# q of two batches loaded in runs of four tokens, with the scores and exponentials that undo the order

## The chip, the cores and the metric

The kernel runs on one core of one Trainium2 chip. The metric is the device time of one execution in microseconds, as the median over several runs. The engines are TensorE (matmuls, PE in the profile; its weight loads are PEld), VectorE (DVE), ScalarE (ACT), GpSimd (POOL) and SyncE (SP, which here only issues DMAs).

## The reference

Sliding-window attention with a linear distance bias, then a two-layer network with a hard swish. Batch 8, 8 heads, 576 tokens, head size 64; the network goes 512 to 2048 to 512 over 4608 tokens.

```python
def _attn_ref(q, k, v):
    B, H, S, D = q.shape                       # 8, 8, 576, 64
    scores = 1.0 / np.sqrt(D) * np.matmul(q, k.transpose(0, 1, 3, 2))
    rel = np.arange(S)[:, None] - np.arange(S)[None, :]
    slopes = 2.0 ** (-8.0 * (np.arange(H) + 1) / H)
    bias = slopes[:, None, None] * (-np.abs(rel))[None]
    mask = (rel >= 0) & (rel < 128)
    scores = np.where(mask, scores + bias[None], -1e9)
    attn = np.exp(scores - scores.max(-1, keepdims=True))
    return np.matmul(attn / attn.sum(-1, keepdims=True), v)

def _moe_ref(x, w_in, w_out):                  # x: (4608, 512), heads side by side
    h = x @ w_in
    return (h * np.clip(h + 3.0, 0.0, 6.0) / 6.0) @ w_out
```

q, k, v and the weights come as float32, the result is float32.

## The kernel before

**Work.** Attention runs in 32 groups: group g is batch g // 4 and one pair of heads, g % 4. The network runs in 9 blocks of 512 tokens; of each, 16 up steps (four matmuls into `hps`, L562, or eight half as wide, then a Relu on ScalarE, L581, and a product on VectorE, L582, into `gbuf`) and 16 down steps (four matmuls into `ops`, L619; after four steps a copy, L628, and a store). The up steps of a block wait for the attention of its tokens. `hps` has two PSUM banks, `ops` one, the attention values `av` one, and the scores `sce` the two tiles of two banks that are left.

**Order.** Every engine runs its instructions in the order in which they are written. Until group 13 a script names each step (`SCRIPT`: `ldq:3:1` loads block 1 of q of batch 3, `ct:3:q` casts it, `xb:3:q` transposes it, `S:12` is the scores of group 12, `ed` and `eo` the exponentials, `v` the values, `F` one step of the network). After that a loop over `slot(g)` writes the scores of group g, then two exponentials of the diagonal, the values of group g - 1, the exponentials beside the diagonal, with network steps between them.

**How q gets to the scores.** From batch 3 on, q (and from batch 4 on, k) is loaded as tokens by SP (`load_tokens`, L140): block j of 128 tokens goes to `ldbuf`, one token to a partition, in eight runs of 256 B, one for each head. The fifth block has the last 64 tokens. GpSimd casts each block to bf16 into `tbuf` (`cast_tokens`, L222), two heads to a pair. SP then transposes all of it by one DMA (`xbar`, L227) into `qTb`: on the partitions the 64 values of two heads, in the columns the 576 tokens of a pair of heads.

**Scores and probabilities.** The scores of a group are taken transposed, keys on the partitions. For each block j of 128 keys, tile `sce[e]` (one for each head of the pair) holds 256 columns: the 128 queries of the same block ("s = 0", the diagonal) and the 128 of the next one ("s = 1"). So that nothing outside the window is computed, each block of keys is cut in four strips of 32, and each strip has a matmul with the 160 queries that can see it (L393; fewer at the end of the sequence), in a tile of 64 x 32 of the array, of which eight run side by side. The last 64 keys have two strips (L400). ScalarE takes the exponentials: of the diagonal into `pd` (L417), of the next block into `po` (L441) and of the last 64 queries' diagonal into `p4buf` (L446); its bias carries the distance term of the key. GpSimd clears what lies outside the window with `affine_select` (L434, L443, L449), which counts columns as tokens. The matmuls of `values` (L462, L470) take `pd`, `po` and `p4buf` as weights, column by column a token. Batches 0 and 1 go other ways, and group 8 has wider score matmuls (L365, L370).

Of the kernel before, what the change touches and what calls it, by code (L numbers as in the profile page):

```python
# [14 lines left out]
ACT = mybir.ActivationFunctionType  # L15
# [3 lines left out]
def kernel(  # L19
# [9 lines left out]
    nc = tc.nc  # L29
    B, H, S, D = q.shape  # L30
# [4 lines left out]
    scale = 1.0 / (D ** 0.5)  # L35
    NP = H // 2
    NQ = 5
    LAST = S - 4 * 128
# [23 lines left out]
    bias_d = perm.tile([128, H], FP32)  # L62
# [23 lines left out]
    src_of = {"q": q, "k": k, "v": v}  # L86
# [43 lines left out]
    def tokens(b, nm):  # L130
        if (b, nm) not in ld:
            i = 2 + b % 2 if b < 3 else (3, 1, 0, 2)[(3 * (b - 3) + "qkv".index(nm)) % 4]
            ld[b, nm] = ldbuf[i][:, 0:NQ * H * D].rearrange("p (j h d) -> p j h d", j=NQ, h=H)
        return ld[b, nm]

    def load_tokens(b, nm, blocks=range(NQ), eng=nc.sync):
        t = tokens(b, nm)
        for j in blocks:
            n = min(128, S - j * 128)
            eng.dma_start(out=t[:n, j, :, :],  # L140
                              in_=src_of[nm][b, :, ds(j * 128, n), :].rearrange("h p d -> p h d"))

# [65 lines left out]
    def staged(b, nm):  # L208
        return tbuf[int(b > 3 and nm == "k")]

    def cast_tokens(b, nm):
        s = ld[b, nm]
        if nm == "v":
            for lo in (0, 2):
                nc.gpsimd.tensor_copy(  # L215
                    out=vbuf[b % 2][:, lo:lo + 2, :, 0:D].rearrange("p j h d -> p (j h) d"),
                    in_=s[:, lo:lo + 2, :, :].rearrange("p j h d -> p (j h) d"))
            nc.gpsimd.tensor_copy(out=vbuf[b % 2][:LAST, 4, :, 0:D], in_=s[:LAST, 4, :, :])
            return
        for j in range(NQ):  # L220
            m = min(128, S - j * 128)
            nc.gpsimd.tensor_copy(out=staged(b, nm)[:m, :, j, :],  # L222
                                  in_=s[:m, j, :, :].rearrange("p (i e) d -> p i (e d)", e=2))

# [5 lines left out]
    st = {}  # L230
# [59 lines left out]
    def full(g):  # L290
        return g < NB_FULL * NP

    def diag_tabled(g):
        return g < NP
# [9 lines left out]
    def rooms(g):  # L304
        b, hp = divmod(g, NP)
        if full(g):
            room = w_out_sb if b == 0 else gbuf[1]
            for i, nm in enumerate(("pd", "po")):
                st[g, nm] = room[:, ds(4 * hp + 2 * i, 2), :].rearrange(
                    "p e (j c) -> p e j c", j=4)  # L310
        else:
            st[g, "pd"] = ppool.tile([128, 2, 4, 128], BF16, tag="pd", name="pd")
            st[g, "po"] = ppool.tile([128, 2, 4, 128], BF16, tag="po", name="po")

    def scores_diag(g):
        rooms(g)
        b, hp = divmod(g, NP)
        qT, kT = qTb[b % 2][:, hp, :, :], kTb[b % 2][:, hp, :, :]
        first = not diag_tabled(g)
        if (g, "scd") not in st:  # L320
            tables_diag(g)
        scd = st[g, "scd"]
        for j in range(4):
            for e in range(2):
                r = slice(e * D, (e + 1) * D)
                nc.tensor.matmul(scd[:, e, ts(j, 128)], lhsT=kT[r, j, :],  # L326
                                 rhs=qT[r, j, :], start=first, stop=first or j == 3)
# [15 lines left out]
    def scores_off(g):  # L343
        b, hp = divmod(g, NP)
        qT, kT = qTb[b % 2][:, hp, :, :], kTb[b % 2][:, hp, :, :]
        foff = not full(g)
        if (g, "sco") not in st:
            tables_off(g)
        sco = st[g, "sco"]
        for e in range(2):  # L350
            r = slice(e * D, (e + 1) * D)
            nc.tensor.matmul(sco[:, e, 64:128], lhsT=kT[r, 4, :],
                             rhs=qT[r, 4, 0:LAST], start=foff, stop=foff)
        for j in range(4):
            n = 128 if j < 3 else LAST
            for e in range(2):
                r = slice(e * D, (e + 1) * D)
                nc.tensor.matmul(sco[:, e, ds((j + 1) % 4 * 128, n)], lhsT=kT[r, j, :],
                                 rhs=qT[r, j + 1, 0:n], start=foff, stop=foff or j == 3)
    def scores_whole(kT, qT, sce):  # L360
        for j in range(4):
            for e in range(2):
                r = slice(e * D, (e + 1) * D)
                n = min(256, S - 128 * j)
                nc.tensor.matmul(  # L365
                    sce[e][:, j, :, :].rearrange("p s c -> p (s c)")[:, 0:n],
                    lhsT=kT[r, j, :], rhs=qT[r, ds(128 * j, n)], start=True, stop=True)
        for e in range(2):
            r = slice(e * D, (e + 1) * D)
            nc.tensor.matmul(sce[e][:, 3, 1, 64:128], lhsT=kT[r, 4, :], rhs=qT[r, 512:S],  # L370
                             start=True, stop=True)

    def scores(g):
        if full(g):
            scores_diag(g)
            scores_off(g)
            return
        rooms(g)
        b, hp = divmod(g, NP)
        qT = qTb[b % 2][:, hp, :, :].rearrange("p j c -> p (j c)")  # L380
        kT = kTb[b % 2][:, hp, :, :]
        if g == 2 * NP:
            st["sce"] = [ps_sc.tile([128, 4, 2, 128], FP32, tag="sc", name="sce")
                         for _ in range(2)]
            scores_whole(kT, qT, st["sce"])
            return
        sce = st["sce"]
        for j in range(4):
            for lo in range(0, 128, 32):
                n = min(160, S - 128 * j - lo)  # L390
                for e in range(2):
                    r = slice(e * D, (e + 1) * D)
                    nc.tensor.matmul(  # L393
                        sce[e][lo:lo + 32, j, :, :].rearrange("p s c -> p (s c)")[:, ds(lo, n)],
                        lhsT=kT[r, j, lo:lo + 32], rhs=qT[r, ds(128 * j + lo, n)],
                        start=True, stop=True)
        for lo in range(0, LAST, 32):
            for e in range(2):
                r = slice(e * D, (e + 1) * D)
                nc.tensor.matmul(sce[e][lo:lo + 32, 3, 1, 64 + lo:128],  # L400
                                 lhsT=kT[r, 4, lo:lo + 32], rhs=qT[r, 512 + lo:S],
                                 start=True, stop=True)
# [10 lines left out]
    def exp_diag(g, e):  # L413
        h = 2 * (g % NP) + e
        pd = st[g, "pd"]
        if not full(g):
            nc.scalar.activation(out=pd[:, e, :, :], in_=st["sce"][e][:, :, 0, :],  # L417
                                 func=ACT.Exp, bias=bias_d[:, h:h + 1], scale=scale)
            mask_diag(g, e)
            return  # L420
        sc = st[g, "scd"]
        if diag_tabled(g):
            if e == 0:
                nc.scalar.activation(out=pd.rearrange("p e j c -> p e (j c)"), in_=sc,
                                     func=ACT.Exp, scale=scale)
            return
        nc.scalar.activation(out=pd[:, e, :, :].rearrange("p j c -> p (j c)"),
                             in_=sc[:, e, :], func=ACT.Exp,
                             bias=bias_d[:, h:h + 1], scale=scale)
        mask_diag(g, e)  # L430
# [7 lines left out]
    def exp_off(g, e):  # L438
        h = 2 * (g % NP) + e
        po, sc, p4 = st[g, "po"], st["sce"][e], p4buf[g % 2]  # L440
        nc.scalar.activation(out=po[:, e, :, :], in_=sc[:, :, 1, :], func=ACT.Exp,  # L441
                             bias=bias_o[:, h:h + 1], scale=scale)
        nc.gpsimd.affine_select(out=po[:, e, :, :], in_=po[:, e, :, :],  # L443
                                pattern=[[0, 4], [-1, 128]], channel_multiplier=1, base=-1,
                                compare_op=ALU.is_ge, fill=0.0)
        nc.scalar.activation(out=p4[:, e, 0:64], in_=sc[:, 3, 1, 64:128], func=ACT.Exp,  # L446
                             bias=bias_d[:, h:h + 1], scale=scale)
        if e == 1:
            nc.gpsimd.affine_select(out=p4[:, :, 0:64], in_=p4[:, :, 0:64],  # L449
                                    pattern=[[0, 2], [1, 64]], channel_multiplier=-1, base=0,  # L450
                                    compare_op=ALU.is_ge, fill=0.0)
# [190 lines left out]
    at = [0]  # L642
# [236 lines left out]
```

## Time and profile before

| | |
|---|---|
| median of 3 runs | 319.1 us (318.49 to 319.7) |
| the profiled execution's own time | 318.45 us |
| its span, first to last instruction | 316.7 us |
| granted TensorE clock | 1.0 throughout |
| busy share of the span | PE 97%, PEld 52%, DVE 56%, ACT 61%, POOL 44% |
| read from and written to memory | 36.70 MB, 9.44 MB |

The profile is of one execution. Busy times count overlapping instructions of an engine once; a matmul's own duration is longer than the step to the next one, as matmuls are pipelined. A row of instructions reads: line, engine, operation, output<-inputs, shape, xcount | busy us, mean ns of one | idle us before them and what ended it. A row of the timeline starts with the start and the duration in us, and merges neighbours of one kind; a bracket at its end would be idle time before it and what ended that. A row of waits has the total, the number and the longest. A row of the chain in order of time has start and duration. In the slices each digit is the busy tenth of 1/40 of the span. A row of DMA issues ends with the KB of one and the median us from issue to landing (a transpose's row shows only the latter).

### The profile page before, as it was taken

The numbers are of one execution on the slowest core, as the hardware profiler recorded it, in microseconds if no ns is written. First come the engines' busy times: TensorE is split into PE (matmuls) and PEld (weight loads), VectorE is DVE, ScalarE is ACT, GpSimd is POOL, SyncE is SP. The second block draws the span as 40 slices with busy tenths as digits, with TensorE's granted clock in tenths as the row PEclk, the third lists the DMA queues.
The fourth block names the chain that finished last, engine by engine and source line by source line (L and its number), as shares of the span: only waits on it lengthen the run. The fifth ranks groups of instructions, "written<-read, shape, count | busy, mean of one in ns | idle before, by whom it ended". The sixth has DMA issues, their size and how long they took to land.

```text
span 316.7 us, 7831 instructions
## 1 busy us (share of the span) xinstructions
PE 308.1 (97%) x3143; PEld 165.7 (52%) x3143; DVE 177.2 (56%) x345; ACT 193.9 (61%) x331; POOL 139.3 (44%) x246
## 2 busy tenths in 40 slices
PE   7879999999999999999999999999999999999996
PEld 6565465555555455544677644455444444444443
DVE  6667585666645655565565556555656455455510
ACT  3758968866857766776677666766774244244401
POOL 8455493456777377636763676363230000000000
PEclk9999999999999999999999999999999999999999
DMA  7999999999999999999999999932212100000112
GB/s 279 198 331 221 265 256 198 232 249 195 184 176 212 213 222 245 227 231 224 207 207 216 205 206 204 218 94 56 57 41 70 54 34 35 33 33 35 66 59 73
DMA packets 131428, 51.95 MB, mean 164 GB/s; under 512 B 118976, under 2 KB 123328, under 8 KB 131392
## 3 DMA queue, kind: packets, MB, share of 16 engines
q1 hardware_dynamic: 126160, 45.36, 69.2%
q0 software_dynamic: 4224, 4.19, 8.3%
q10 hardware_dynamic: 1008, 1.90, 1.7%
q8 instruction: 24, 0.39, 0.5%
q14 instruction: 12, 0.10, 0.1%
HBM read 36.70 MB, written 9.44 MB: 146 GB/s over the span
## 4 chain that ended last, share of the span: by engine, by line
PE 90%; DMA 3%; DVE 2%; POOL 2%; ACT 1%; SPq 1%; issue 0%; POOLq 0%
PE hps L562 39%; PE ops L619 39%; PE sce L393 3%; DMA ldbuf<-in_q_dram 3%; PE av L470 2%; PE av L462 2%; PE tp L261 1%; PE ops L593 1%; DVE avs L493 1%; DVE gbuf L582 1%; PE sco L337 1%; PE scd L326 1%; SPq L126 1%; PE tp L246 0%; ACT w_out_sb L405 0%
## 5 line engine op out<-in xcount | busy, mean ns | idle before, releaser
L581 ACT ACTIVATE r<-hps,bias 128x512 f32<-128x512 f32 x144 | 99.0, 689 | 88.7 <-PE hps L562 88.5
L582 DVE SCALAR_TENSOR_TENSOR gbuf<-r,hps 128x512 bf16<-128x512 f32 x144 | 98.7, 687 | 94.6 <-ACT r L581 93.2
L562 PE MATMUL hps<-xT,w_in_sb 128*128 128x512 bf16 (+1 forms) x640 | 144.4, 358 | 0.3 <-ACT xT L549 0.3
L619 PE MATMUL ops<-w_out_sb,gbuf 128*128 128x512 bf16 x560 | 138.3, 379 | 0.0
L562 PEld LDWEIGHTS <-w_in_sb 128*128 128x128 bf16 x640 | 59.4, 98 | 55.1 <-DMA w_in_sb<-in_moe_w_in_dram 0.4
L619 PEld LDWEIGHTS <-gbuf 128*128 128x128 bf16 x560 | 51.7, 98 | 55.3
L443 POOL TENSOR_SCALAR_AFFINE_SELECT po<-po 128x512 bf16<-128x512 bf16 x48 | 30.5, 637 | 44.4 <-ACT po L441 44.4
L434 POOL TENSOR_SCALAR_AFFINE_SELECT pd<-pd 128x512 bf16<-128x512 bf16 x48 | 29.9, 635 | 31.9 <-ACT pd L417 31.8
L417 ACT ACTIVATE pd<-sce,bias_d 128x512 bf16<-128x512 f32 x48 | 31.8, 685 | 5.6 <-POOL tbuf L222 3.9
L628 DVE COPY osb<-ops 128x512 f32<-128x512 f32 x33 | 22.7, 687 | 22.3 <-PE ops L619 22.2
L441 ACT ACTIVATE po<-sce,bias_o 128x512 bf16<-128x512 f32 x48 | 32.9, 686 | 0.1
L222 POOL CAST tbuf<-ldbuf 128x512 bf16<-128x512 f32 (+1 forms) x45 | 25.6, 615 | 0.1
L481 DVE TENSOR_TENSOR avs<-av,rc 128x384 bf16<-128x384 f32 (+1 forms) x48 | 23.5, 490 | 1.6
L470 PEld LDWEIGHTS <-pd 128*128 128x128 bf16 x192 | 14.3, 97 | 7.4 <-POOL pd L434 0.2
L462 PE MATMUL av<-vbuf,po 128*128 128x65 bf16 x192 | 18.0, 193 | 0.0
L470 PE MATMUL av<-vbuf,pd 128*128 128x65 bf16 x192 | 17.3, 194 | 0.0
L462 PEld LDWEIGHTS <-po 128*128 128x128 bf16 x192 | 14.4, 98 | 2.4
L446 ACT ACTIVATE p4buf<-sce,bias_d 128x64 bf16<-128x64 f32 x48 | 15.4, 321 | 0.0
L253 POOL CAST pr<-ldbuf 128x576 bf16<-128x576 f32 x16 | 10.5, 672 | 7.2 <-DMA ldbuf<-in_k_dram 5.3
L215 POOL CAST vbuf<-ldbuf 128x1024 bf16<-128x1024 f32 x12 | 12.2, 1044 | 2.3 <-DMA ldbuf<-in_v_dram 2.3
L393 PEld LDWEIGHTS <-kTb 64*32 64x32 bf16 x736 | 6.2, 91 | 8.3 <-issue 8.1
L393 PE MATMUL sce<-qTb,kTb 64*32 64x160 bf16 (+1 forms) x736 | 10.5, 229 | 0.0
(104 smaller groups left out, 215.1 us busy)
## 6 DMA issues: line engine op xcount, KB each, us to landing
out_dram<-osb SPq DMA_DIRECT2D x33, 256.0 KB, 2.9
ldbuf<-in_v_dram SPq DMA_DIRECT2D x32, 256.0 KB, 4.9
ldbuf<-in_q_dram SPq DMA_DIRECT2D x20, 256.0 KB, 5.0
ldbuf<-in_k_dram SPq DMA_DIRECT2D x16, 256.0 KB, 4.5
ldbuf<-in_q_dram SPq DMA_DIRECT2D x12, 288.0 KB, 6.8
ldbuf<-in_k_dram SPq DMA_DIRECT2D x12, 288.0 KB, 6.2
w_in_sb<-in_moe_w_in_dram POOLq DMA_DIRECT2D x4, 512.0 KB, 9.4
w_out_sb<-in_moe_w_out_dram POOLq DMA_DIRECT2D x4, 512.0 KB, 10.5
```

The source lines that it names most:

```text
L222: nc.gpsimd.tensor_copy(out=staged(b, nm)[:m, :, j, :], in_=s[:m, j, :, :].rearrange("p (i e) d -> p i (e d)", e=2))
L393: nc.tensor.matmul(sce[e][lo:lo + 32, j, :, :].rearrange("p s c -> p (s c)")[:, ds(lo, n)], lhsT=kT[r, j, lo:lo + 32], rhs=qT[r, ds(128 * ...
L417: nc.scalar.activation(out=pd[:, e, :, :], in_=st["sce"][e][:, :, 0, :], func=ACT.Exp, bias=bias_d[:, h:h + 1], scale=scale)
L434: nc.gpsimd.affine_select(out=pd[:, e, :, :], in_=pd[:, e, :, :], pattern=[[0, 4], [1, 128]], channel_multiplier=-1, base=0, compare_op=AL ...
L441: nc.scalar.activation(out=po[:, e, :, :], in_=sc[:, :, 1, :], func=ACT.Exp, bias=bias_o[:, h:h + 1], scale=scale)
L443: nc.gpsimd.affine_select(out=po[:, e, :, :], in_=po[:, e, :, :], pattern=[[0, 4], [-1, 128]], channel_multiplier=1, base=-1, compare_op=A ...
L462: nc.tensor.matmul(out_av, lhsT=po[:, e, qt % 4 if full(g) else qt - 1, :], rhs=vb[:, qt - 1, h, :], start=True, stop=False)
L470: nc.tensor.matmul(out_av, lhsT=d, rhs=vb[:, qt, h, :], start=(qt == 0), stop=True)
L562: nc.tensor.matmul(hps[:, lo:hi], lhsT=w_in_sb[:, ks, ts(ms, 128)], rhs=xT[:, ks, ds(src, hi - lo)], start=(ks == 0), stop=(ks == n_ks - 1))
L581: nc.scalar.activation(out=r6, in_=hps, func=ACT.Relu, bias=bias3[:, 0:1], scale=1.0 / 6.0)
L582: nc.vector.scalar_tensor_tensor(out=gts[nt][:, ms, :], in0=r6, scalar=1.0, in1=hps, op0=ALU.min, op1=ALU.mult)
L619: nc.tensor.matmul(ops[nt, sub], lhsT=gts[nt][:, ms, ts(sub, 128)], rhs=w_out_sb[:, ms, :], start=(ms == 0), stop=(ms == n_ms - 1))
```

## The change

For batches 3 and 4, blocks 0 to 3 of q are loaded differently. DMA j now brings heads 2j and 2j + 1, and partition a gets tokens 4a to 4a + 3 of each, which lie together in memory: two runs of 1 KB for a partition. The cast takes block j to head pair j, ordered by token within the four, then head. After the transpose, the first 512 columns of `qTb` are ordered t, a for token 4a + t. The fifth block (64 tokens) is loaded, cast and transposed as before.

The scores read q^T by fours: a strip's queries are four runs of up to 40 columns, and go to four runs of the 256 columns of its block in `sce`, where a column now stands at t x 64 + a. Queries from 512 on, which lie in token order, are read every fourth column to the same layout, in matmuls of their own: 44 matmuls to a group, where there were 36. The exponentials read `sce` as a, t, neighbours 64 float32 apart, and write `pd`, `po` and `p4buf` in token order, so that masks and values stay as they are. The script and the order of the steps are unchanged.

```diff
+    FOURS = (3, 4)
+
+    def by_fours(b, nm):
+        return b in FOURS and nm == "q"
+
     def load_tokens(b, nm, blocks=range(NQ), eng=nc.sync):
         t = tokens(b, nm)
         for j in blocks:
             n = min(128, S - j * 128)
+            if by_fours(b, nm) and j < 4:
+                eng.dma_start(out=t[:, j, :, :].rearrange("p (e t) d -> p e (t d)", e=2),
+                              in_=src_of[nm][b, 2 * j:2 * j + 2, 0:512, :].rearrange(
+                                  "e (a t) d -> a e (t d)", t=4))
+                continue
             eng.dma_start(out=t[:n, j, :, :],
                               in_=src_of[nm][b, :, ds(j * 128, n), :].rearrange("h p d -> p h d"))
 ...
+            if by_fours(b, nm) and j < 4:
+                nc.gpsimd.tensor_copy(
+                    out=staged(b, nm)[:, j, 0:4, :].rearrange("p t (e d) -> p t e d", e=2),
+                    in_=s[:, j, :, :].rearrange("p (e t) d -> p t e d", e=2))
+                continue
 ...
+    def fours(ap):
+        return ap.rearrange("p (a t) -> p t a", t=4)
+
+    def scores_fours(kT, qT, sce):
+        q4 = qT[:, 0:512].rearrange("p (t a) -> p t a", t=4)
+
+        def block(e, j, lo, at, src):
+            r = slice(e * D, (e + 1) * D)
+            to = sce[e][lo:lo + 32, min(j, 3), :, :].rearrange(
+                "p s c -> p (s c)").rearrange("p (t a) -> p t a", t=4)
+            nc.tensor.matmul(to[:, :, ds(at, src.shape[-1])], lhsT=kT[r, j, lo:lo + 32],
+                             rhs=src[r], start=True, stop=True)
+
+        for j in range(4):
+            for lo in range(0, 128, 32):
+                n = min(160, 512 - 128 * j - lo)
+                for e in range(2):
+                    block(e, j, lo, lo // 4, q4[:, :, ds((128 * j + lo) // 4, n // 4)])
+        for lo in range(0, 128, 32):
+            for e in range(2):
+                block(e, 3, lo, 32, fours(qT[:, ds(512, min(32 + lo, LAST))]))
+        for lo in range(0, LAST, 32):
+            for e in range(2):
+                block(e, 4, lo, 48 + lo // 4, fours(qT[:, 512 + lo:S]))
+
+    def part(sc, g, s):
+        if g // NP not in FOURS:
+            return sc[:, :, s, :]
+        return sc.rearrange("p j s c -> p j (s c)").rearrange(
+            "p j (t a) -> p j a t", t=4)[:, :, ds(32 * s, 32), :]
+
+    def whole(out, g):
+        return out if g // NP not in FOURS else out.rearrange("p j (a t) -> p j a t", t=4)
 ...
-            nc.scalar.activation(out=pd[:, e, :, :], in_=st["sce"][e][:, :, 0, :],
+            nc.scalar.activation(out=whole(pd[:, e, :, :], g), in_=part(st["sce"][e], g, 0),
                                  func=ACT.Exp, bias=bias_d[:, h:h + 1], scale=scale)
 ...
-        nc.scalar.activation(out=po[:, e, :, :], in_=sc[:, :, 1, :], func=ACT.Exp,
+        nc.scalar.activation(out=whole(po[:, e, :, :], g), in_=part(sc, g, 1), func=ACT.Exp,
                              bias=bias_o[:, h:h + 1], scale=scale)
 ...
-        nc.scalar.activation(out=p4[:, e, 0:64], in_=sc[:, 3, 1, 64:128], func=ACT.Exp,
-                             bias=bias_d[:, h:h + 1], scale=scale)
+        nc.scalar.activation(out=whole(p4[:, e:e + 1, 0:64], g),
+                             in_=part(sc[:, 3:4, :, :], g, 1)[:, :, 16:32, :] if g // NP in FOURS
+                             else sc[:, 3:4, 1, 64:128], func=ACT.Exp, bias=bias_d[:, h:h + 1], scale=scale)
```

More of the change, by code (lines that the diff above doesn't have):

```diff
@@ L387, in scores @@
         sce = st["sce"]
+        if b in FOURS:
+            scores_fours(kT, qT, sce)
+            return
         for j in range(4):
```

## The prediction

> **What bounds the kernel now.** I read the slices of the page and its chain first, then what TensorE waited for in the part of the run that the change touches.
>
> ```profile
> PE   7879999999999999999999999999999999999996
> ACT  3758968866857766776677666766774244244401
> DMA  7999999999999999999999999932212100000112
> PE 90%; DMA 3%; DVE 2%; POOL 2%; ACT 1%; SPq 1%; issue 0%; POOLq 0%
> ```
>
> TensorE and the DMA engines are both full from slice 2 to slice 26, so both are candidates. The chain says which: 90% of it is TensorE and 3% is DMA. I place that 3% next. Asked for the waits of TensorE's matmuls from 50 us to the end, the view names none; for its weight loads it names three:
>
> ```profile
> PEld L393 <- issue: 8.1, 20, 0.4
> PEld L562 <- issue: 0.2, 1, 0.2
> PEld L470 <- POOL pd L434: 0.2, 1, 0.2
> ```
>
> No DMA and no q among them. "Issue" is no wait on another engine (the weight loads of the scores get ahead and sit there), so 0.2 us, behind a mask, is all the waiting for somebody else. The DMA share is one early stretch, long before:
>
> ```profile
> 14.75 8.04 DMA ldbuf<-in_q_dram
> ```
>
> When do the changed parts run? The timeline gives the first and last of the eight score groups of batches 3 and 4, the q cast of batch 3, and its transpose:
>
> ```profile
> 72.57 2.84 POOL L222 CAST tbuf<-ldbuf 128x512 bf16<-128x512 f32 x5
> 75.44 3.42 SPq L227 DMA_TRANSPOSE qTb<-tbuf  x1
> 83.17 0.46 PE L393 MATMUL sce<-qTb,kTb 64*32 64x160 bf16 x32
> 134.99 0.46 PE L393 MATMUL sce<-qTb,kTb 64*32 64x160 bf16 x32
> sum 64.00, PE 64.00 PEld 32.39 DVE 35.68 ACT 44.86 POOL 42.03; mean PE 8.00 PEld 4.05 DVE 4.46 ACT 5.61 POOL 5.25
> ```
>
> The last row sums eight stretches of 8 us from 83 to 147 us: TensorE busy 64.00 of 64.00, ScalarE 5.61 of each 8. So in this stage the matmul stream itself sets the end. What the change takes off the DMA queues buys nothing; what it adds to TensorE is paid in full; what it adds to ScalarE is paid only where a matmul comes to wait for it.
>
> **The loads.** The eight changed q loads (four blocks of two batches, 128 x 8 runs of 256 B each) have 8,192 packets; as 1 KB runs they have 2,048.
>
> ```profile
> DMA packets 131428, 51.95 MB, mean 164 GB/s; under 512 B 118976, under 2 KB 123328, under 8 KB 131392
> q1 hardware_dynamic: 126160, 45.36, 69.2%
> q0 software_dynamic: 4224, 4.19, 8.3%
> ```
>
> A packet of q1, nearly all of 256 B, takes 0.692 x 16 x 316.7 us / 126,160 = 27.8 ns. One of q0, about 1 KB, takes 0.083 x 16 x 316.7 / 4,224 = 99.6 ns. Between a 1 KB packet at 99.6 and at 27.8 ns the change frees (8,192 x 27.8 - 2,048 x 99.6)/16 = 1.5 us to 6,144 x 27.8/16 = 10.7 us on each DMA engine. Worth in time: nothing, as no matmul here waits for a transfer. The loads keep their places in SP's queue; what stands behind them there (other loads, transposes, stores) can only issue earlier if the loads are quicker. Were one slower, the cover is this: the five casts at 72.57 ran without waiting for a DMA.
>
> **The cast and the transpose.** The cast keeps five instructions of 128x512. Its input goes from flat to runs of 64, its output from four runs to one. Rows for both kinds, and the transposes' landing:
>
> ```profile
> L222 POOL CAST tbuf<-ldbuf 128x512 bf16<-128x512 f32 x36 | 20.6, 616 | 0.0
> L218 POOL CAST vbuf<-ldbuf 64x512 bf16<-64x512 f32 x6 | 3.7, 613 | 2.4 <-DMA ldbuf<-in_v_dram 2.4
> qTb<-tbuf SPq DMA_TRANSPOSE x5, 6.9
> ```
>
> L218 writes runs of 64 (65 apart) and takes 613 ns against 616, so I take no change. The transpose of batch 3, issued at 75.44, should land near 82.3, 0.8 us ahead of the first score group at 83.17; the cast may grow by 0.8 us (a quarter) before that group waits. Groups follow each other every (134.99 - 83.17)/7 = 7.4 us, so batch 4's first scores come 30 us later, and its q is loaded right behind this transpose: there the room is wider.
>
> **The scores.** One old group among the dense matmuls:
>
> ```profile
> 126.06 1.03 PE L562 MATMUL hps<-xT,w_in_sb 128*128 128x512 bf16 x4
> 127.02 0.46 PE L393 MATMUL sce<-qTb,kTb 64*32 64x160 bf16 x32
> 127.31 0.19 PE L400 MATMUL sce<-qTb,kTb 64*32 64x64 bf16 x4
> 127.43 1.04 PE L619 MATMUL ops<-w_out_sb,gbuf 128*128 128x512 bf16 x4
> ```
>
> A group has 36 matmuls; the new one has 44, because block 3's queries split into those of the fours and the last 64. The columns are the same: per head 3 x 4 x 160 + (160 + 160 + 128 + 96) + 96 = 2,560 before, 1,920 + (128 + 96 + 64 + 32) + (32 + 64 + 64 + 64) + 96 = 2,560 after. The 32 take 127.31 - 127.02 = 0.29 us, 9 ns each, so eight more cost between nothing (columns decide) and 0.072 us (count decides): over eight groups 0 to 0.6 us. A gain is excluded, as nothing is removed. I take the middle, 0.3 us, since block 3's short pieces leave parts of the array unequally loaded. That the outputs now go to four runs of 40 columns, and some inputs are read every fourth element, no row shows; the trace has no matmul with a broken output. From below it costs 0, from above I take a doubling (rival two).
>
> **The exponentials.** They read PSUM in runs of four, neighbours 256 B apart, to write token order. There is a near row: ScalarE's copies of transposes read PSUM just so (neighbours 128 bf16, 256 B, apart), in runs of 9, 5 or 4.
>
> ```profile
> L441 ACT ACTIVATE po<-sce,bias_o 128x512 bf16<-128x512 f32 x48 | 32.9, 686 | 0.1
> L549 ACT COPY xT<-tb 128x576 bf16<-128x576 bf16 x6 | 3.9, 647 | 4.0 <-PE tb L544 4.0
> L405 ACT ACTIVATE gbuf<-sco 128x1024 bf16<-128x1024 f32 x4 | 4.1, 1026 | 0.1
> L286 ACT COPY qTb<-tp 128x1152 bf16<-128x1152 bf16 x1 | 1.1, 1119 | 0.0
> L274 ACT COPY kTb<-tp 128x640 bf16<-128x640 bf16 x4 | 3.0, 753 | 1.7 <-PE tp L261 1.7
> L274 ACT COPY kTb<-tp 128x512 bf16<-128x512 bf16 x2 | 1.4, 720 | 0.0
> L446 ACT ACTIVATE p4buf<-sce,bias_d 128x64 bf16<-128x64 f32 x48 | 15.4, 321 | 0.0
> ```
>
> The flat reads L549 and L405 give (1026 - 647)/448 = 0.846 ns per element, so flat would be 1134 at 1152, 701 at 640, 593 at 512. Runs of 9 (L286) took 1119: the stride alone costs nothing. Runs of 5 took 753, +52; runs of 4 took 720, +127. The new exponentials have 128 runs of 4, as the last row has, so +0.13 us each (686 to 815 ns), with 0 as the lower end (the excess could come from L274's broken output; the new output is flat). p4's 16 runs add 16 ns to 321. Per group 4 x 0.13 + 2 x 0.016 = 0.55 us, 4.4 us over eight groups; ScalarE goes from 5.61 to 6.2 of each 8 us. The Trainium skill speaks against this edit: "Advanced Engine Details and Errata", section PSUM Cachelines, says every two consecutive elements should be contiguous for best throughput, and these never are. The L286 row disagrees, as it ran at the flat rate with neighbours 256 B apart.
>
> Does a matmul come to wait? The tightest places, in order of time:
>
> ```profile
> 96.17 0.32 ACT L446 ACTIVATE p4buf<-sce,bias_d 128x64 bf16<-128x64 f32 x1
> 96.88 0.46 PE L393 MATMUL sce<-qTb,kTb 64*32 64x160 bf16 x32
> 129.96 0.68 ACT L417 ACTIVATE pd<-sce,bias_d 128x512 bf16<-128x512 f32 x1
> 130.53 0.69 ACT L441 ACTIVATE po<-sce,bias_o 128x512 bf16<-128x512 f32 x1
> 131.40 0.69 ACT L581 ACTIVATE r<-hps,bias 128x512 f32<-128x512 f32 x1
> 132.12 0.69 DVE L582 SCALAR_TENSOR_TENSOR gbuf<-r,hps 128x512 bf16<-128x512 f32 x1
> 133.17 1.03 PE L562 MATMUL hps<-xT,w_in_sb 128*128 128x512 bf16 x4
> ```
>
> The next scores overwrite the PSUM tiles that the last exponential read: 96.49 to 96.88 leaves 0.39 us. And an up-projection reuses the bank that VectorE left at 132.81: 0.36 us ahead of 133.17. At that second place two exponentials and one p4 run back to back ahead of the Relu, together 0.28 us late: about 0.1 us is left, near what a semaphore takes. So at 0.13 us I get no stall. I carried longer ones through the rows of the eight groups (each instruction starts at its old time, or when what precedes it on its engine or what it waits for is done): the stalls add up to 0.5 us at 0.20 per exponential, 1.3 at 0.25, 2.1 at 0.30 and 4.6 at 0.43. The edge is near 0.13.
>
> **The sum.** Loads 0, casts 0, scores +0.3, exponentials 0 on the path. The profiled execution took 318.45 us (1.75 outside its span of 316.7), so 318.75; the median of the runs, 319.1, is 0.65 above that execution, so the median after is 319.4.
>
> **The rivals.** One, slower by ScalarE: reading fp32 in runs of four costs more than the bf16 copies show. It decides from about 0.27 us per exponential; at 0.30 the sum is +2.4 us, 321.5; at half rate (+0.43, 512 more element times at 0.846) +4.9, 324.0. For: fp32 is no row there. Against: L286's full rate. Chance 0.16.
>
> Two, slower by TensorE: broken outputs double the score rounds, 8 x 0.29 = 2.3 us more, 321.7. Nothing in the trace excludes it. The Trainium skill, "PSUM — Partial Sum Buffer", Specifications, says that any non-contiguous pattern slows matmuls significantly; no run here shows it, and runs of 160 bytes break it only at their ends. Chance 0.08.
>
> Three, faster: the freed DMA time counts after all, by easing the traffic beside TensorE's reads. By the chain:
>
> ```profile
> 145.57 1.73 PE ops L619 x8
> 299.79 10.36 PE ops L619 x48
> ```
>
> Eight in 1.73 us amid full DMA and 48 in 10.36 us with hardly any are both 216 ns each. There is nothing to ease. If all of the least saving, 1.5 us, came off, 317.6. Chance 0.03.
>
> Four: the run stays split in 256 B packets; then the loads change nothing and the time is the forecast's. Chance 0.02. The forecast itself has 0.71.
>
> **How the numbers follow.** About 0.5% (1.6 us) is what a measurement can tell from no change. Same: forecast and rival four, and 0.02 of rival one below its point, 0.75 in all, of which I give 0.03 to sums just over the bound: 0.72. Faster 0.03, slower 0.25. The range starts 0.9 below the old median (the runs spread 1.2 us) and goes up to 322.2, which holds rivals one at 0.30 and two, and leaves out only the half rate.
>
> **What would show it.** Right: total packets down by 6,144, those under 512 B by 8,192; 64 more score matmuls; the 32 exponentials near 815 ns; still no wait of a matmul past 50 us. Wrong: score groups spanning 0.6 us or more, exponentials above 0.9 us with matmuls of the scores (on L446) or of the up-projection (on L582) waiting between 83 and 147 us, or a cast over 0.75 us.

## The result and the profile after

The changed kernel takes 320.95 us (median; 319.95 to 321.96) against 318.84 us of the kernel before: ratio 1.0065, interval 1.0047 to 1.0083. It lies inside the stated range, but on its slower side, past the bound of 0.5% (which the interval still reaches); the forecast itself was 319.4. The profiled execution took 320.95 us, its span is 319.2, 2.5 us more than before.

The page after: packets, fetches of instructions, and the chain.

```profile
DMA packets 125285, 51.97 MB, mean 163 GB/s; under 512 B 110784, under 2 KB 117184, under 8 KB 125248
q8 instruction: 25, 0.41, 0.6%
PE 84%; DMA 6%; DVE 3%; POOL 2%; issue 2%; ACT 1%; POOLq 0%
```

The loads do what they say: 8,192 fewer small packets, 6,143 fewer in all (6,144 and one more fetch of instructions). The chain has lost TensorE's share, and part of it went to DMA. The waits of TensorE's matmuls from 50 us on, none before, are now:

```profile
PE ops L672 <- issue: 1.8, 11, 0.2
PE hps L615 <- DMA xT<-avs: 1.4, 2, 0.7
PE hps L615 <- issue: 0.2, 1, 0.2
```

"Issue" is gaps in the records: 42 of 3,207 matmuls are missing in this profile, none in that of before. The second row is real: twice an up step waits for a transpose into xT, the attention output that the network reads. The timeline has the two places, the first and last score group of batches 3 and 4, and one of them among its neighbours:

```profile
83.40 0.56 PE L398 MATMUL sce<-qTb,kTb 64*32 64x160 bf16 x44
127.72 0.56 PE L398 MATMUL sce<-qTb,kTb 64*32 64x160 bf16 x44
135.77 0.56 PE L398 MATMUL sce<-qTb,kTb 64*32 64x160 bf16 x44
155.91 1.14 PE L615 MATMUL hps<-xT,w_in_sb 128*128 128x256 bf16 x9 [0.74 <-DMA xT<-avs]
188.61 1.24 PE L615 MATMUL hps<-xT,w_in_sb 128*128 128x512 bf16 x5 [0.62 <-DMA xT<-avs]
```

From the first to the last score group it is 52.37 us, against 51.82 before: 0.55 over seven groups, 0.079 us each, so 0.6 us for eight. The two waits have 1.4 us. The first score group starts 0.23 us later than before, a difference that is there at 30 us already, while the first changed load is issued at 61 us, so that no edit reaches it. 0.6 + 1.4 + 0.2 = 2.2 of the 2.5 us. The other 0.3 comes at the two waits, which cost more than the idle time that the rows show: from the score group before each to the one behind it, the stream falls back by 0.90 and 0.78 us against before.

ScalarE and GpSimd, grouped by shape, between 83 and 147 us (the last row over the whole run):

```profile
L469 ACT ACTIVATE pd<-sce,bias_d 128x512 bf16<-128x512 f32 x18 | 12.0, 684 | 1.8 <-PE sce L398 1.8
L493 ACT ACTIVATE po<-sce,bias_o 128x512 bf16<-128x512 f32 x16 | 11.0, 685 | 0.0
L498 ACT ACTIVATE p4buf<-sce,bias_d 128x64 bf16<-128x64 f32 x17 | 5.5, 321 | 0.0
L233 POOL CAST tbuf<-ldbuf 128x512 bf16<-128x512 f32 x8 | 4.6, 612 | 0.0
```

The exponentials that pick single elements 256 B apart out of PSUM take 684 to 685 ns, what the flat ones took; the casts take 612.

### The profile page after: what moved, and what is told of

Its sections match the earlier page's. It is cut to its first block, busy times and chain, and to the rows that moved or that the text cites. A ratio compares the mean times of both kernels' runs of the same rounds, so it can differ in the third digit from the quotient of the medians.

```text
span 319.2 us, 7917 instructions
## 1 busy us (share of the span) xinstructions
PE 304.6 (95%) x3165; PEld 165.5 (52%) x3207; DVE 177.6 (56%) x345; ACT 194.1 (61%) x331; POOL 139.1 (44%) x246
## 4 chain that ended last, share of the span: by engine, by line
PE 84%; DMA 6%; DVE 3%; POOL 2%; issue 2%; ACT 1%; POOLq 0%
PE hps L615 37%; PE ops L672 36%; DMA w_in_sb<-in_moe_w_in_dram 3%; DMA xT<-avs 3%; PE av L523 2%; PE av L515 2%; PE sce L445 2%; PE sce L398 1%; PE ops L646 1%; DVE avs L546 1%; PE tp L276 1%; PE scd L341 1%; PE sco L352 1%; DVE gbuf L635 1%; DVE kTb L262 1%
## 5 line engine op out<-in xcount | busy, mean ns | idle before, releaser
L672 PE MATMUL ops<-w_out_sb,gbuf 128*128 128x512 bf16 x533 | 134.0, 379 | 2.5 <-issue 1.8
L237 POOL CAST tbuf<-ldbuf 128x512 bf16<-128x512 f32 (+1 forms) x37 | 21.1, 615 | 0.0
L533 DVE RECIPROCAL rc<-av 128x6 f32<-128x6 f32 (+1 forms) x48 | 8.7, 182 | 1.7 <-PE av L523 1.7
L276 PE MATMUL tp<-ident,pr 128*128 128x128 bf16 x90 | 7.4, 219 | 0.2
```

Of the source, the lines that this page charges most:

```text
L672: nc.tensor.matmul(ops[nt, sub], lhsT=gts[nt][:, ms, ts(sub, 128)], rhs=w_out_sb[:, ms, :], start=(ms == 0), stop=(ms == n_ms - 1))
```

## The experiments

A first guess is that the loads, having become other traffic, hold up the transposes (theory A of the first four runs); the rival is that the wait comes with what is added to the scores. The first four kernels part the change.

**Loads alone.**

```diff
         sce = st["sce"]
-        if b in FOURS:
-            scores_fours(kT, qT, sce)
-            return
...
-            nc.scalar.activation(out=whole(pd[:, e, :, :], g), in_=part(st["sce"][e], g, 0),
+            nc.scalar.activation(out=pd[:, e, :, :], in_=st["sce"][e][:, :, 0, :],
```

> Only the loads and the casts of q of batches 3 and 4 go by fours; scores and exponentials are those of before, so the order is not put back and the output of these two batches is of mixed tokens. Theory A (the loads move the DMA traffic so that the transposes into xT land later and the up-projection waits for them): no step in the score groups, but stalls before the up steps that need batches 4 and 5, about 1.5 us in all, ratio 1.004 to 1.005, and a spread of the runs as wide as that of after (2 us). Theory B (the loads are hidden and the stalls come with TensorE's added time): ratio 1.000, no wait of a matmul for xT.

Measured: 319.0 us, ratio 0.9969 (0.9952 to 0.9986). One wait for xT of 0.68 us at 155 us, none near 188. Theory A falls: the loads by themselves cost nothing, and perhaps bring 0.3%, beyond what theory B expected (which had no wait for xT either). Its profile does not show from where; the kernel of before ran at 0.9989 on the same chip (below), so a part of it may be the chip's scatter.

**Scores and exponentials alone.**

```diff
     def by_fours(b, nm):
-        return b in FOURS and nm == "q"
+        return False
```

> Only the scores and exponentials go by fours; q is loaded and cast as before, so the scores read wrong queries and the output of batches 3 and 4 is not the reference's. Both theories: eight steps of 0.08 us in the PE stream, one at each group, 0.62 us. Theory A: nothing more, ratio 1.002. Theory B: the stalls for xT as well, ratio 1.006.

Measured: 322.51 us, ratio 1.0083 (1.0053 to 1.0113). Waits for xT of 0.93 us at 158.7 and 0.65 us at 191.4. So the second wait and at least a part of the loss come with this half. Not all of it: the profiled execution (323.8 us) is 2.8 us behind that of before at 30 us already, where no edit is, and the runs spread from 320.53 to 325.29.

**Before and after once more,** unchanged.

> The kernel of before, unchanged. If the stalls for xT are chance of an execution and not of the change, this profile can show one too and its runs spread by 1.5 us or more; if they belong to the change, ratio 1.000 and no matmul waits for xT.

Measured: 319.58 us, ratio 0.9989 (0.9968 to 1.001). One wait for xT, at 155.3 us, 0.94 us; none near 188. The place at 155 us is therefore on the edge in the kernel of before as well: the first profile of it had no wait there, this one has.

> The changed kernel again. Ratio 1.0065 and again 0.62 us in eight steps; if the stalls for xT are a matter of single executions, they stand at other places or have another size in this profile than the 0.74 and 0.62 us of the first one, with the same 0.62 us of steps.

Measured: 321.87 us, ratio 1.0063 (1.0039 to 1.0088). Waits of 1.75 us at 157.1 and 0.61 us at 189.8. The second wait is the same as in the first profile to 0.01 us: it is no chance. What makes it? The transpose itself is longer. The DMA view of the stretch in which the last transpose of batch 5 is in flight, before (182 to 185.1 us) and after (184 to 188.6 us); the last number of the xT row is the time from issue to landing:

```profile
q1 hardware_dynamic: 1118, 0.50, 68.2%
q14 instruction: 1, 0.01, 0.6%
xT<-avs SPq DMA_TRANSPOSE x1, 2.8
```

```profile
q1 hardware_dynamic: 2661, 0.78, 73.6%
q8 instruction: 1, 0.02, 1.4%
xT<-avs SPq DMA_TRANSPOSE x1, 4.6
```

In after, a packet of queue q8 lies inside. q8 fetches instructions, 16 KB at a time: 24 fetches before, 25 after, one about every 256 instructions of TensorE (6,286 matmuls and weight loads before, 6,414 after: the 64 matmuls added and their 64 weight loads). q14 fetches instructions too, 8 KB at a time and in about 0.3 us; one of its packets lies in four of the six short flights of the table below, so such a packet does not by itself lengthen a flight so far. So a new theory A: the count of instructions shifts the points of the fetches, and one now falls into this flight. Theory B keeps to the strided work or the later start of the groups. The next four kernels part these.

**64 matmuls more, far away from the change.** In groups 9 and 10 of the kernel of before, at 57 to 72 us, the strips' first 32 columns are computed twice.

```diff
+        if g in (9, 10):
+            for j in range(4):
+                for lo in range(0, 128, 32):
+                    for e in range(2):
+                        r = slice(e * D, (e + 1) * D)
+                        nc.tensor.matmul(sce[e][lo:lo + 32, j, 0, lo:lo + 32],
+                                         lhsT=kT[r, j, lo:lo + 32],
+                                         rhs=qT[r, ds(128 * j + lo, 32)], start=True, stop=True)
```

> The kernel of before with 64 matmuls more in groups 9 and 10 alone: each strip's first 32 columns are computed a second time into the same place, which changes nothing in the values. Nothing of batches 3 and 4 is touched. Theory A (the added matmul instructions move the points at which TensorE's instruction stream is fetched, one 16 KB fetch for every 256 instructions, and a fetch now falls into the flight of the transposes that the up-projection waits for): steps of 0.1 to 0.3 us at groups 9 and 10, then the wait for xT near 188 us that after, after_again and scores_only had (0.6 us), its transpose in flight 4.5 us with a fetch inside, ratio 1.003 to 1.004. Theory B (the wait comes from the strided score or exponential work, or from the later start of the groups of batches 3 and 4): the two steps, no wait near 188 us, ratio 1.001.

Measured: 322.02 us, ratio 1.0094 (1.0066 to 1.0123), no less than the whole change costs. The 32 repeated matmuls take 0.27 us a group. The timeline's waits:

```profile
124.62 1.24 PE L570 MATMUL hps<-xT,w_in_sb 128*128 128x512 bf16 x5 [1.55 <-DMA xT<-avs]
157.73 1.14 PE L570 MATMUL hps<-xT,w_in_sb 128*128 128x256 bf16 x9 [0.95 <-DMA xT<-avs]
190.41 0.81 PE L570 MATMUL hps<-xT,w_in_sb 128*128 128x512 bf16 x3 [0.60 <-DMA xT<-avs]
```

And the DMA view from 185.7 to 190.4 us:

```profile
q8 instruction: 1, 0.02, 1.3%
xT<-avs SPq DMA_TRANSPOSE x1, 4.5
```

The wait of 0.6 us stands there again, with a fetch in the flight, in a kernel whose batches 3 and 4 are those of before. A third place, at 124.6 us, was not expected; there too a fetch, at 122.3 us, lies in the flight of the transpose, issued at 119.3, which takes 5.3 us (3.1 in before). Theory B cannot explain this; the size is over theory A's 1.004, by that third wait.

**The same 64 on top of the change.** With the 64 of the change they make 256 instructions, one whole fetch.

```diff
     (the changed kernel, with the block above in groups 9 and 10)
```

> The changed kernel with the same 64 repeated matmuls in groups 9 and 10: with the 64 of the change that is 256 instructions (a matmul and a weight load each), so from group 19 on the fetches fall where they fell before, one fetch later. Theory A: eight steps of 0.08 us, 0.2 to 0.5 us at groups 9 and 10, and no wait near 188 us, its transpose in flight about 3 us; the wait near 155 us as in before (0 to 0.9 us); ratio 1.003 to 1.004, below after's 1.0065 though it does more. Theory B: the wait near 188 us stays, ratio 1.008.

Measured: 319.6 us, ratio 1.0021 (1.0006 to 1.0035). No row of a matmul waiting for xT is left anywhere after 50 us, and from 183.3 to 186.1 us:

```profile
q1 hardware_dynamic: 1071, 0.48, 66.2%
q14 instruction: 1, 0.01, 0.7%
xT<-avs SPq DMA_TRANSPOSE x1, 2.7
```

A kernel that does strictly more than the changed one, 0.5 us of useless matmuls, takes less time than it. The wait at 155 us is gone in this profile as well.

**The split alone.** Ordinary loads and exponentials, token order, but block 3's strips cut at query 512 in batches 3 and 4.

```diff
-                n = min(160, S - 128 * j - lo)
+                n = min(160, (512 if b in (3, 4) else S) - 128 * j - lo)
...
+        for lo in range(0, 128, 32) if b in (3, 4) else ():
+            for e in range(2):
+                r = slice(e * D, (e + 1) * D)
+                n = min(32 + lo, LAST)
+                nc.tensor.matmul(sce[e][lo:lo + 32, 3, 1, 0:n], lhsT=kT[r, 3, lo:lo + 32],
+                                 rhs=qT[r, ds(512, n)], start=True, stop=True)
```

> The kernel of before with only the split of block 3's strips at query 512 in the groups of batches 3 and 4: 44 matmuls to a group in the order of after, but all reading in token order, ordinary exponentials and loads. It parts the 0.078 us step of a group into the count of matmuls and the reading of every fourth element. If the count makes the step, 0.07 to 0.08 us a group; if the half-rate reading (214 against 189 ns for 64 columns) makes it, 0.03 to 0.04. Theory A besides: the wait near 188 us of 0.6 us, as the fetches stand as in after; ratio 1.003 to 1.005. Theory B (strided work is what causes the wait): none, ratio 1.001 to 1.002.

Measured: 321.08 us, ratio 1.0075 (1.005 to 1.0099), with waits for xT of 1.14 us at 156.2 and 0.35 us at 188.7. First and last group:

```profile
83.44 0.44 PE L393 MATMUL sce<-qTb,kTb 64*32 64x160 bf16 x32
135.72 0.44 PE L393 MATMUL sce<-qTb,kTb 64*32 64x160 bf16 x32
```

52.28 us apart, 0.46 more than before, 0.066 us a group: the count makes five sixths of the step, strided reading and the broken outputs together the other 0.013. With nothing strided at all, the waits are there.

**A phase that should miss both flights.** The changed kernel, with the strips of the last queries in another order, and wide scores in group 11.

```diff
-        for lo in range(0, 128, 32):
+        for lo in (96, 64, 32, 0):
             for e in range(2):
                 block(e, 3, lo, 32, fours(qT[:, ds(512, min(32 + lo, LAST))]))
...
+        if g == 11:
+            scores_whole(kT, qT, sce)
+            return
```

> The changed kernel with two edits: the strips of the last 64 queries of block 3 are issued from the lowest-loaded part of the array on (strips 96, 64, 32, 0), and group 11 takes its scores in ten wide matmuls where it had 36. That is 52 instructions fewer ahead of batch 3, so the fetches stand 76 instructions earlier than in before and, at about 47 ns for an instruction, near 146 and 176 us, outside both flights. Expected: steps of about 0.05 us a group, 0.1 to 0.15 us at group 11, neither wait, so the median of before or up to 0.2% under it, ratio 0.998 to 1.001. Theory B: the waits stay, ratio 1.005.

Measured: 321.21 us, ratio 1.0056 (1.0031 to 1.0081). A miss, in two ways. The order of the strips made the groups longer, near 0.1 us each and not 0.05. And of the two waits one is gone, at 155 us, but the other is there:

```profile
189.18 1.02 PE L618 MATMUL hps<-xT,w_in_sb 128*128 128x512 bf16 x4 [2.20 <-DMA xT<-avs]
```

The DMA view from 184.6 to 189.2 us has the reason:

```profile
q8 instruction: 1, 0.02, 1.3%
xT<-avs SPq DMA_TRANSPOSE x1, 4.5
```

The fetches stood at 146.5 and 177.2 us, as worked out, but the one after them at 186.5: 256 instructions take 8 us in one stretch and 14 in another, and 47 ns for each was too coarse. The wait follows the fetch, not the intent. It is 2.20 us here, where after had 0.62, because the stream, having lost nothing near 155 us, comes 1.0 us earlier than in after, while the transpose is issued 0.6 us later (184.65 against 184.01).

**Both kernels with fetches near 147 and 188 us.** Read off the fetch times so far, not from a mean.

```diff
     (the kernel of before)
+        for i in range(24 if g == 9 else 0):
+            j, lo, e = i // 8, i // 2 % 4 * 32, i % 2
+            r = slice(e * D, (e + 1) * D)
+            nc.tensor.matmul(sce[e][lo:lo + 32, j, 0, lo:lo + 32], lhsT=kT[r, j, lo:lo + 32],
+                             rhs=qT[r, ds(128 * j + lo, 32)], start=True, stop=True)
```

> The kernel of before with 24 repeated matmuls in group 9, 48 instructions. Read from the fetch times of the kernels so far (48 fewer to go put a fetch about 2.5 us earlier near 150 us and 4 to 5 us earlier near 193), fetches should stand near 147.5 and 188, outside the flights of both transposes. Theory A: 0.2 us of step, neither wait, so the 0 to 0.9 us that before loses near 155 us comes back; ratio 0.997 to 1.000. Theory B: ratio 1.001, wait near 155 us as in before_again.

Measured: 320.08 us, ratio 1.002 (0.9993 to 1.0046). The profiled execution shows what was expected: fetches at 145.9 and 189.7 us, no wait for xT, a span of 316.9. The median does not, and theory A's ratio is missed: it is not faster than before. Its runs spread from 318.12 to 321.68, the profiled one (318.57) is among the fastest, and what the slower ones wait for is open.

```diff
     (the changed kernel)
+        for i in range(13 if g == 9 else 0):
+            (as above)
...
+        if g in (10, 11):
+            scores_whole(kT, qT, sce)
+            return
```

> The changed kernel with its fetches at the same places as in before_moved: groups 10 and 11 take their scores in ten wide matmuls (104 instructions fewer), and 13 matmuls are repeated in group 9 (26 more), so that batch 5 starts 50 instructions later in the count than in before. Theory A: steps of 0.62 us in batches 3 and 4, 0.3 at groups 10 and 11, 0.1 at group 9, neither wait; ratio 1.001 to 1.003. Theory B: the waits of after on top, ratio 1.009.

Measured: 319.51 us (318.64 to 319.86), ratio 1.0003 (0.9983 to 1.0023). All that TensorE waits for from 50 us on:

```profile
PE ops L680 <- issue: 1.8, 11, 0.2
PE hps L623 <- issue: 0.2, 1, 0.2
```

And the last transpose of batch 5, 183.4 to 186.4 us:

```profile
q1 hardware_dynamic: 1079, 0.49, 66.2%
q14 instruction: 1, 0.01, 0.7%
xT<-avs SPq DMA_TRANSPOSE x1, 2.8
```

The change as it stands, with 1.0 us of matmul time more than the kernel of before, takes the same time as that kernel. It undoes the loss and gains nothing beyond. The only version below the kernel of before by more than its interval is the loads alone, at 0.9969.

Over the twelve profiles, the flight of that transpose and the wait behind it:

| kernel | fetch within the flight | issue to landing, us | wait near 188 us |
|---|---|---|---|
| before, before_again, loads_only | none | 2.8, 3.0, 3.0 | none |
| repeat_after2, before_moved, after_moved | none | 2.7, 2.7, 2.8 | none |
| after, after_again, scores_only | one | 4.6, 4.6, 4.6 | 0.62, 0.61, 0.65 |
| repeat_before2, split_only2, after_tuned2 | one | 4.5, 4.3, 4.5 | 0.60, 0.35, 2.20 |

The three profiles with a fetch that were not meant to test it, and the three that were, agree; moving the fetch in (repeat_before2) and out (repeat_after2, after_moved) moves the wait, with no edit near it. That the fetch decides over this wait is shown.

The place at 155 us fits the same rule, with one transpose more: two of batch 4 land ahead of it, one behind the other. In five profiles a fetch lies in the second (after, after_again, scores_only, repeat_before2, split_only2; its flight is 4.5 to 4.8 us, against 2.6 to 3.4 without), and all five wait there, 0.74 to 1.75 us. In four it lies in the first (the two of before, loads_only, repeat_after2; 5.2 to 5.3 us, against 3.2 to 3.6 without), and two of these wait. In three it lies in neither (before_moved, after_moved, after_tuned2), and none waits.

How a fetch lengthens the flight by 1.7 us is not shown. It is one packet, which took 0.014 x 16 x 4.6 = 1.0 us in the window of after above, on one of the 16 engines. When it comes matters: for the four transposes issued between 214 and 244 us, where little else moves, the flights without a fetch are 2.6 to 2.8 us, those with one that begins 0.4 to 0.7 us after the issue 2.9 to 3.6, 2.1 to 2.2 us after it 4.2 to 4.3, and later than that 2.6 again. The Trainium skill, "DMA: Bandwidth & Descriptors", section "Queues, rings and completion order", has each engine change between queues only at the end of a packet, and its section "Why a DMA increments its semaphore by 16 and not by 1" has a DMA landed only when all its engines are done. By these two and the measured packet, a transpose with a share on that engine would lose up to 1.0 us, an estimate; the traces have 0.7 us more.

## Why the prediction was right or wrong

**The bound.** Right for the kernel of before: TensorE's stream sets the end from 50 us on, and everything that was lost is added work or waits of that stream. "What the change takes off the DMA queues buys nothing" held in direction for the whole change; loads_only leaves room for up to 0.5%, which the profile before does not explain.

**Loads, cast, transpose of q.** Right: the packets as counted, casts of 612 against 616 ns, no score group waiting for q.

**Scores.** The mechanism was right, the term was mis-sized: 0.3 us was taken out of 0 to 0.6, and it is 0.079 x 8 = 0.6, the upper end. The working there had columns against count; split_only2 says count, 0.066 of the 0.079 us. The doubling for broken outputs (rival two) did not happen: a whole group with them is 0.013 us longer than one of split_only2 without, where doubling would add 0.29. The rows of after say the same (the profile models the ends of matmuls): the 160-column matmuls with four runs in the output take 233 ns, those with one run 232:

```profile
L398 PE MATMUL sce<-qTb,kTb 64*32 64x160 bf16 x192 | 3.2, 233 | 0.0
L445 PE MATMUL sce<-qTb,kTb 64*32 64x160 bf16 x28 | 0.5, 232 | 0.0
L398 PE MATMUL sce<-qTb,kTb 64*32 64x64 bf16 x80 | 2.6, 209 | 0.0
L452 PE MATMUL sce<-qTb,kTb 64*32 64x64 bf16 x2 | 0.2, 189 | 0.0
```

The last two rows point to a small cost of strided reading: 209 ns on the mean for 64 columns, eight in ten of them read every fourth element, against 189. On outputs of runs of 40 the page of the Trainium skill that rival two named ("PSUM — Partial Sum Buffer", Specifications) is not borne out.

**Exponentials.** Wrong by 0.13 us each: they cost nothing. The choice between the ends failed: the excess of L274 was put down to its input in runs of four. The lower end had another reason for it, its broken output; that is what is left, but no run tests it. Since the sum had no stall at 0.13 us either, the total did not suffer. Rival one is out. The Trainium skill's rule in "Advanced Engine Details and Errata", PSUM Cachelines, is not borne out for ScalarE's reads here: 684 to 685 ns with neighbours 256 B apart, 685 to 686 flat.

**Still no wait of a matmul.** This is the step that failed. The waits were searched among those who wait for ScalarE, because that is where work was added. That no matmul waited for a DMA past 50 us was read from one execution, while the second profile of the same kernel has 0.94 us at 155. The room that the transposes into xT had was not looked at: in the first profile of before the second of batch 4 landed 0.36 us ahead of its matmul, and the last of batch 5, issued at 182.24 and 2.83 us in flight, landed at 185.07, 0.99 us ahead of its own, which is the fourth of the eight in the second row:

```profile
182.24 1.20 SPq L536 DMA_TRANSPOSE xT<-avs  x1
185.41 1.89 PE L562 MATMUL hps<-xT,w_in_sb 128*128 128x512 bf16 x8
```

In after its issue moved with the stream, 1.77 us later (184.01). A flight of 4.56 us instead of 2.83 uses up the 0.99 and 0.74 more; the stream falls back by 0.78 there. The count of instructions was priced by its time alone. It has a second price: where in the program the next 16 KB are fetched. The 1.4 us of waits in the profile are more than all that the sum held. The chance of 0.25 for slower was on mechanisms of which none took place, and the range held the measured time only because it made room for them: that part is luck.

## What to carry to other kernels

In a kernel whose transfers land within a microsecond of their use, look at the landing times of every DMA that the bound engine reads, also of those that the change doesn't touch, before calling a wait impossible. An edit that adds or removes some dozen instructions on TensorE moves the instruction fetches of everything behind it; before crediting or blaming the edit, add the same count of idle instructions elsewhere and compare. The median of such a kernel is worth little without the list of its waits.

## What the runs showed of the hardware that was not expected

In these profiles TensorE's instructions come in 16 KB fetches on a DMA queue, 24 or 25 to an execution, one per about 256 instructions, each about 1 us on an engine. With one of them inside, the last DMA transpose of batch 5 (160 KB) took 4.3 to 4.6 us instead of 2.7 to 3.0. At other places and phases the difference is smaller, and a fetch is not the only thing that counts: transposes without one took up to 4.6 us.

ScalarE read fp32 from PSUM in runs of four with neighbours 256 B apart at the flat rate (684 to 685 ns for 512), and TensorE wrote 160 columns in four separate runs in 233 ns, in one run in 232. Reading the moving operand (the queries) every fourth bf16 seems to cost a little: 64 columns in 209 ns on the mean instead of 189.
